# Attention woven into an expert layer on one core: key copies, exponentials and weight splits moved in the program order

## The chip, the cores and the metric

One core of a Trainium2 chip runs the whole kernel. Its engines are TensorE (PE, whose weight loads the profile lists apart as PEld), VectorE (DVE), ScalarE (ACT), GpSimd (POOL) and SyncE (SP, which here only issues DMA transfers). Each engine works through its own queue in order; semaphores tie the queues together. The metric is the device time of one execution in microseconds (us), as the median of several runs.

## The reference

Three layers follow each other (shapes: 4 batches, 8 heads, 768 positions, head size 64; 3072 tokens of 512 numbers; hidden size 2048; 8 experts of 4 slots):

```python
scores_l = scale * q @ k.T            # only |i - j| < 16 counts, the rest is masked with -1e9
scores_s = scale * q @ k_sum.T + log(32)   # k_sum: maximum of each block of 32 keys (24 blocks)
a = softmax(concat[scores_l, scores_s])
attn = a @ concat[v, v_sum]           # v_sum: mean of each block of 32 values

h = x @ w_in                          # 512 -> 2048, x = attn of all heads
g = h * cos(h)
x2 = g @ w_out                        # 2048 -> 512

logits = x2 @ phi
d = softmax(logits, over tokens);  c = softmax(logits, over slots)
out = c @ experts(d.T @ x2)           # per expert: relu(. @ w1) @ w2
```

## The kernel before

Attention is cut into 24 groups of four query windows of 64 positions and four heads (lines 622 to 650 place groups 4 to 23; groups 0 to 3 are written out ahead of the loop). The middle layer is cut into 6 blocks of 512 tokens, and each block into 16 steps of 128 hidden columns, so the main loop (line 689) has 96 steps s = 0 to 95. Four attention groups give one block's input. Block 0 needs groups 0 to 3, which run in the prologue; groups 4 to 7 run inside block 0, groups 8 to 11 inside blocks 0 and 1, and so on.

**One step.** Every product is in split form: a number is a high part that TensorE takes exactly plus a low rest. `mm1(s)` (lines 340 to 352) makes 12 matmuls of 512 columns into the PSUM tile `h`: the high weights `wih` with both parts of the input (`xh`, `xl`), then the low weights `wil` with `xh`. `act1(s)` (line 355) turns h into the cosine: two DVE operations on the tile `a` (L365, L366) and the sine on ACT (L367). `act2(s)` multiplies by h on DVE (L372), casts the high part `gh` on ACT (L375) and subtracts the low part `gl` on POOL (L376). `mm2(s-2)` (lines 379 to 393) multiplies `gh`, `gl` with the output weights `woh`, `wol`, 12 matmuls again. TensorE's queue is therefore mm1(s), mm2(s-2), mm1(s+1), mm2(s-1), with attention's small matmuls between them.

**Weights.** Both splits of step s are made by `split_w` (lines 330 to 337): a cast on ACT (L335), a subtraction on POOL (L336; in block 0 on DVE for `wi`). In block 0 each weight must first be converted from 64-bit floats: two ACT operations into `w` and `cv` (`conv_1`, L123 and L127), a shift on DVE (`conv_2`, L133), an integer addition on POOL (`conv_3`, L138).

**Attention of a group g.** `att_K` (L227) copies the block maxima of the keys `ks` behind the keys in the tile `qk`, twice 96 columns on ACT. `att_A` makes 32 score matmuls `sc` (L250) into two PSUM banks and adds scale and mask on DVE into `S` (L254). Then come the maximum (L262), the exponential, the sum, the division (`att_norm`, L290 to L293), two rounds of four transposes `tr` (`att_C`, L300) with a copy `aT` each, and `att_D`: 32 matmuls `av` (L317) whose result is split into `xh` (ACT) and `xl` (DVE). Groups 8 to 23 subtract the maximum on DVE (L266) and use one exponential for a pair of groups (`att_exp`, L271, 1920 columns). Groups 0 to 7 use `att_exps` (L283): eight exponentials of 120 columns for each group, each with its own bias and accumulated sum.

**What sets the order.** The order is written by hand. Line 690 on lists, for each step: mm1, in block 0 the conversion of a later weight, the split of `wo`, act1, the split of `wi`, what is due at position 0, act2, mm2, what is due at position 1. `at2(h, ...)` files a piece of attention under half-step h = 2s + position; the constants at the top (`HB`, `HF`, `OK`, `MC` and others) say how many half-steps a piece lies behind its group's start. All scores, transposes, `av` and block sums of values (`vs`, L181) inside the loop share two PSUM banks (the pool `ps_m`), taken in turn: a tile gets the bank of the last but one, and its first matmul waits until that one has been read. The tile `aT` has two buffers too.

Of the kernel before, what the change touches and what calls it, by code (L numbers as in the profile page):

```python
# [32 lines left out]
NF = DFF // 128  # L33
# [14 lines left out]
NRING = 7  # L48
HB = (0, 12)
HF = (-6, 10)  # L50
OA = 4
OV = 3
OK = 0
OX = 6
# [9 lines left out]
ML = 12  # L64
MC = 2
MS = 22
# [8 lines left out]
def body(ctx: ExitStack, tc: tile.TileContext, q0, qk, kT, vn, vx, w, phi, ex, cst, out):  # L75
# [187 lines left out]

    def att_sub(g):
        d = grp[g]
        nc.vector.tensor_tensor(out=d["S"], in0=d["S"],  # L266
                                in1=d["mx"].unsqueeze(2).to_broadcast([128, 8, KC]), op=ALU.subtract)
# [259 lines left out]
    def turn(g, eng=None):  # L527
        for j in range(2):
            att_C(g, j, eng or nc.vector)
# [39 lines left out]
    vsum_first()  # L569
    load_vs(0)  # L570
    load_vs(2)
    load_w(2)
    att_exps(3)
    fill(8)
    turn(0)
    load_vs(1)
    load_vs(3)
    load_w(3)
    load_qk(4)
    fill(6)  # L580
    conv_1(0)
    load_w(4)
    turn(2)
    att_norm(1, nc.gpsimd)
    fill(6)
    turn(1)
    att_norm(3, nc.gpsimd)
    conv_2(0)
    conv_3(0)
    fill(6)  # L590
    att_D(0)
    turn(3, nc.scalar)
    att_D(2)
    split_w(0, 0, nc.vector)
    att_D(1)
    att_D(3)
    conv_1(1)
    load_w(5)
    conv_2(1)
    conv_3(1)  # L600
    load_qk(5)
    att_K(4)
    split_w(1, 0, nc.vector)
    load_v(4)
    load_v(5)
    load_vs(4)
    load_vs(5)
    load_c(sel, NM + 180, 288)
    nc.sync.dma_start(out=phis.rearrange("p k s -> p (k s)"), in_=phi)

    def convert(f):
        conv_1(f)
        conv_2(f)
        conv_3(f)
        if 4 <= f < NF - 2:
            load_w(f + 2)


    for g in range(4, 24):
        h0 = HF[g // 2 % 2] + 2 * NF * (g // 4 - 1) if g > 7 else HB[g // 2 % 2]  # L620
        h = h0 + OA * (g % 2)
        n = h0 + ON + DN * (g % 2)
        if g < 8:
            if g > 5:
                at2(n - 5, load_v, g)
                at2(n - 4, load_vs, g)
                at2(h - 2, att_K, g)
            elif g == 5:
                at2(h - 1, att_K, g)
        else:  # L630
            v = n - 14 + OD2
            at2(v + 1, load_v, g)
            at2(v + 2, load_vs, g)
            at2(h - OK, att_K, g)
        at2(h, att_A, g)
        if g < 8:
            at2(h + 1, att_max, g, True)
            at2(h0 + OX, att_exps, g)
        else:
            at2(h + 1, att_max, g)  # L640
            at2(h + 1, att_sub, g)
            if g % 2:
                at2(h0 + OX, att_exp, g // 2)
            at2(h0 + OS + 2 * (g % 2), att_sum, g)
        at2(n, att_norm, g)
        at2(n + OC2, att_C, g, 0)
        at2(n + OC2 + 1, att_C, g, 1)
        at2(n + OD2, att_D, g)
        if g + 2 < 24:
            at2(h + 1, load_qk, g + 2)  # L650
# [38 lines left out]
    for s in range(NSLOT + LAG):  # L689
        if s < NSLOT:  # L690
            mm1(s)
        for f in range(2 if s == 0 else s + CL, min(s + CL + 1, NF)):
            convert(f)
        if 0 <= s - LAG + 1 < NSLOT:
            split_w((s - LAG + 1) % NF, 1)
        if s < NSLOT:
            act1(s)
        if s + 2 < NSLOT:
            split_w((s + 2) % NF, 0, nc.vector if s + 2 < NF else None)
        fire(s, 0)  # L700
        if s < NSLOT:
            act2(s)
        if s >= LAG:
            mm2(s - LAG)
            if (s - LAG) % NF == NF - 1:
                last = [x2_out(t) for t in range(4)][3]
        fire(s, 1)
        fire(s, 2)
# [242 lines left out]
```

## Time and profile before

| | us |
|---|---|
| median of 3 runs (870.97 to 871.92) | 871.5 |
| the profiled execution | 871.47 |
| its span, first to last instruction | 869.6 |
| mean granted TensorE clock | 0.94 of full speed |
| PE busy | 752.1 |
| DVE busy | 461.3 |
| ACT busy | 402.8 |
| POOL busy | 400.0 |

The profile is of one execution. Its page lists busy time of each engine, the span in 40 slices, the chain of work that ended last, and the costliest groups of instructions by line; the trace behind it answers what one engine waited for, what ran in a window, and each instruction's start and length. A granted clock of 1.00 is TensorE's 2.4 GHz level and the lower level is 1.2 GHz, so a mean of 0.86 over a window means that it was at the lower level for 28% of it. mm1 of step 0 begins at 38.72 us, of step 16 at 201.58 us, of step 64 at 586.75 us, of step 80 at 702.54 us.

### The profile page before, as it was taken

Reading aid. Unit: us, or ns where it says so; the run is one execution under the profiler, and the core shown is the slowest. Engines: PE = TensorE matmul, PEld = TensorE weight load, DVE = VectorE, ACT = ScalarE, POOL = GpSimd, SP = SyncE. Lnnn points to the kernel's source line nnn. Section 1 sums busy time; section 2 is a strip of 40 time slices with the busy share of each in tenths; the row PEclk is TensorE's granted clock in tenths of the full one; section 3 lists DMA queues with packets and bytes.
Section 4 is the critical chain, followed back from the end, with each engine's and each line's share of the span. In section 5 each row is a group of like instructions: output and inputs, shape, how many; then the busy total and the mean of one; then the engine's idle time right before and its main releaser. Section 6 shows DMA issues by size and latency. Waiting matters only on the chain.

```text
span 869.6 us, 13683 instructions
## 1 busy us (share of the span) xinstructions
PE 752.1 (86%) x5453; PEld 582.5 (67%) x5453; DVE 461.3 (53%) x688; ACT 402.8 (46%) x765; POOL 400.0 (46%) x300
## 2 busy tenths in 40 slices
PE   7847695779979979889979889889889999999995
PEld 6736474567857757767657767667667888877553
DVE  6465664656445547556446446556456544442723
ACT  5467557535524435534435524526425444443312
POOL 1355544534633734543634543746444666574000
PEclk9979799889998999999989989999999999999998
DMA  9775554132111021121111011020000282235978
GB/s 345 264 257 178 218 181 173 48 102 64 54 64 35 29 82 54 65 89 62 51 64 36 30 65 35 29 87 13 30 29 1 77 335 97 74 98 194 376 315 278
DMA packets 36304, 101.71 MB, mean 117 GB/s; under 512 B 3472, under 2 KB 14736, under 8 KB 34192
## 3 DMA queue, kind: packets, MB, share of 16 engines
q1 hardware_dynamic: 36240, 100.83, 32.9%
q8 instruction: 43, 0.70, 0.3%
q14 instruction: 21, 0.17, 0.1%
HBM read 92.17 MB, written 6.29 MB: 113 GB/s over the span
## 4 chain that ended last, share of the span: by engine, by line
PE 65%; DVE 13%; ACT 12%; issue 4%; DMA 3%; POOL 1%; SPq 0%; ACTq 0%; DVEq 0%; POOLq 0%
PE acc L388 10%; PE acc L389 9%; PE h L347 8%; PE acc L392 8%; PE h L348 7%; PE h L351 7%; DVE a L366 3%; DVE a L365 3%; PE sc L250 3%; PE av L317 3%; ACT a L367 2%; ACT wih L335 2%; PE tr L300 2%; PE yp L849 2%; PE hp L816 2%
## 5 line engine op out<-in xcount | busy, mean ns | idle before, releaser
L376 POOL TENSOR_TENSOR gl<-a,gh 128x512 fp32r<-128x512 f32 x96 | 124.1, 1292 | 147.8 <-ACT gh L375 147.8
L336 POOL TENSOR_TENSOR wil<-w,wih 128x512 fp32r<-128x512 f32 x80 | 106.9, 1337 | 175.4 <-ACT wih L335 135.7
L388 PE MATMUL acc<-woh,gh 128*128 128x512 f32 x384 | 169.9, 442 | 1.6 <-ACT gh L375 1.6
L367 ACT ACTIVATE a<-a,halfpi 128x512 f32<-128x512 f32 x96 | 69.5, 724 | 212.6 <-DVE a L366 205.0
L347 PE MATMUL h<-xh,wih 128*128 128x512 f32 x384 | 157.5, 410 | 8.8 <-DVE a L372 7.2
L389 PE MATMUL acc<-wol,gh 128*128 128x512 f32 x384 | 161.5, 420 | 0.0
L348 PE MATMUL h<-xl,wih 128*128 128x512 f32 x384 | 152.5, 397 | 0.1
L336 POOL TENSOR_TENSOR wol<-w,woh 128x512 fp32r<-128x512 f32 x96 | 128.4, 1337 | 27.7 <-ACT woh L335 27.6
L365 DVE TENSOR_SCALAR a<-h 128x512 f32<-128x512 f32 x96 | 66.0, 688 | 126.2 <-PE h L351 97.1
L375 ACT CAST gh<-a 128x512 fp32r<-128x512 f32 x96 | 59.4, 619 | 129.6 <-DVE a L372 129.6
L392 PE MATMUL acc<-woh,gl 128*128 128x512 f32 x384 | 104.7, 395 | 0.0
L351 PE MATMUL h<-xh,wil 128*128 128x512 f32 x384 | 104.3, 394 | 0.0
L388 PEld LDWEIGHTS acc<-woh,gh 128*128 128x128 f32 x384 | 79.4, 207 | 30.2 <-issue 11.5
L347 PEld LDWEIGHTS h<-xh,wih 128*128 128x128 f32 x384 | 73.2, 191 | 26.2 <-issue 8.4
L389 PEld LDWEIGHTS acc<-wol,gh 128*128 128x128 f32 x384 | 79.7, 208 | 16.4 <-issue 0.4
L392 PEld LDWEIGHTS acc<-woh,gl 128*128 128x128 f32 x384 | 74.2, 193 | 17.1
L348 PEld LDWEIGHTS h<-xl,wih 128*128 128x128 f32 x384 | 73.4, 191 | 15.2 <-DVE xl L326 0.5
L351 PEld LDWEIGHTS h<-xh,wil 128*128 128x128 f32 x384 | 72.6, 189 | 16.2
L372 DVE TENSOR_TENSOR a<-h,a 128x512 f32<-128x512 f32 x96 | 65.9, 686 | 29.7 <-ACT a L367 29.5
L250 PE MATMUL sc<-qk 64*64 64x120 f32 x640 | 30.0, 341 | 55.2 <-ACT qk L227 55.2
L366 DVE SCALAR_TENSOR_TENSOR a<-a,h 128x512 f32<-128x512 f32 x96 | 66.0, 688 | 3.3
L250 PEld LDWEIGHTS sc<-qk 64*64 64x64 f32 x640 | 23.6, 176 | 63.4 <-ACT qk L227 62.7
(128 smaller groups left out, 943.5 us busy)
## 6 DMA issues: line engine op xcount, KB each, us to landing
ex<-in_ex_dram SPq DMA_DIRECT2D x64, 512.0 KB
raw<-in_w_dram SPq DMA_DIRECT2D x16, 1024.0 KB
qk<-in_qk_dram SPq DMA_DIRECT2D x20, 736.0 KB
v<-in_vx_dram SPq DMA_DIRECT2D x24, 512.0 KB
kr<-in_kT_dram SPq DMA_DIRECT2D x16, 384.0 KB
vb<-in_vn_dram SPq DMA_DIRECT2D x12, 512.0 KB
out_dram<-o SPq DMA_DIRECT2D x12, 512.0 KB
v<-vs SPq DMA_DIRECT2D x48, 48.0 KB
```

The source lines that it names most:

```text
L250: nc.tensor.matmul(pss[hh][o, c:c + KC], t[:, 0:QB], t[:, QB:], start=True, stop=True)
L336: (eng or nc.gpsimd).tensor_tensor(out=lo, in0=W[f][:, part, :], in1=hi, op=ALU.subtract)
L347: nc.tensor.matmul(h, hi[:, c], xh[s // NF][:, t, :], start=t == 0, stop=False)
L348: nc.tensor.matmul(h, hi[:, c], xl[s // NF][:, t, :], start=False, stop=False)
L351: nc.tensor.matmul(h, lo[:, c], xh[s // NF][:, t, :], start=False, stop=t == 3)
L365: nc.vector.tensor_scalar(out=a, in0=h, scalar1=0.25, scalar2=MAGIC, op0=ALU.add, op1=ALU.add)
L366: nc.vector.scalar_tensor_tensor(out=a, in0=a, scalar=MAGIC, in1=h, op0=ALU.subtract, op1=ALU.subtract)
L367: nc.scalar.activation(a, a, AF.Sin, bias=halfpi, scale=-TWO_PI)
L376: nc.gpsimd.tensor_tensor(out=gl, in0=a, in1=gh, op=ALU.subtract)
L388: nc.tensor.matmul(acc[t], gh[:, c], hi, start=f == 0, stop=False)
L389: nc.tensor.matmul(acc[t], gh[:, c], lo, start=False, stop=False)
L392: nc.tensor.matmul(acc[t], gl[:, c], hi, start=False, stop=f == NF - 1)
```

## The change

- **Key copies** (`att_K`) of groups 8 to 23 are filed three half-steps ahead of their scores (`OK` from 0 to 3). In block 0 those of groups 6 and 7 are too, that of group 5 two half-steps.
- **Activation first.** In every step act1 comes directly behind mm1. The splits of both weights, and in block 0 the conversions, come behind mm2; the output weights of step s are split in step s instead of s+1. A conversion is cut into its ACT half and its DVE and POOL half, one step apart.
- **One exponential per pair** for groups 4 to 7, as groups 8 to 23 have it: the subtraction goes to POOL, the sum to DVE; the pieces are placed anew (`HB` from (0, 12) to (2, 13), and new offsets).
- **Prologue.** The second weight is converted earlier, the normalisations on POOL come earlier, loads are listed in another order, the filler matmuls (`fill`) are dealt out otherwise.
- `MC` from 2 to 3: `m2_c`, the transposition `dt` of the token weights, one half-step later.

```diff
-HB = (0, 12)
+HB = (2, 13)
-OK = 0
+OK = 3
-MC = 2
+MC = 3
...
-    def att_sub(g):
+    def att_sub(g, eng=None):
         d = grp[g]
-        nc.vector.tensor_tensor(out=d["S"], in0=d["S"],
+        (eng or nc.vector).tensor_tensor(out=d["S"], in0=d["S"],
...
+    def convert(f, parts):
+        if 1 in parts and f < NF:
+            conv_1(f)
+            if 4 <= f < NF - 2:
+                load_w(f + 2)
+        if 2 in parts and f < NF:
+            conv_2(f)
+            conv_3(f)
...
         if g < 8:
             if g > 5:
...
+                at2(h - 3, att_K, g)
+            elif g == 5:
                 at2(h - 2, att_K, g)
...
+            at2(h, att_A, g)
+            at2(h + 1, att_max, g)
+            at2(h + 1, att_sub, g, nc.gpsimd)
+            if g % 2:
+                at2(h0 + 7, att_exp, g // 2)
+            n = h0 + 9 + g % 2
+            at2(n, att_sum, g)
+            at2(n + 1, att_norm, g)
+            n = h0 + 12 + 2 * (g % 2)
+            at2(n, att_C, g, 0)
+            at2(n + 1, att_C, g, 1)
+            at2(h0 + 15 + 2 * (g % 2), att_D, g)
         else:
...
-        for f in range(2 if s == 0 else s + CL, min(s + CL + 1, NF)):
-            convert(f)
-        if 0 <= s - LAG + 1 < NSLOT:
-            split_w((s - LAG + 1) % NF, 1)
-        if s < NSLOT:
+            if s == 0:
+                convert(2, (2,))
             act1(s)
-        if s + 2 < NSLOT:
-            split_w((s + 2) % NF, 0, nc.vector if s + 2 < NF else None)
         fire(s, 0)
         if s < NSLOT:
             act2(s)
...
+        if s == 0:
+            convert(3, (1,))
+        if s + 2 < NSLOT:
+            split_w((s + 2) % NF, 0, nc.vector if s + 2 < NF else None)
+        convert(s + 3, (2,))
+        if s < NSLOT:
+            split_w(s % NF, 1)
+        convert(s + 4, (1,))
         fire(s, 1)
```

How the queues change, at the places that matter below. ACT's queue in step 21, in which group 10's scores are made (`a21` is the sine of step 21, `qk10` the key copies of group 10), before:

```order
L335 CAST woh4_2158<-w4_697 128x512
L367 ACTIVATE a21_2162<-a21_2162,halfpi_90 128x512
L335 CAST wih7_2166<-w7_895 128x512
L227 COPY qk10_1663<-ks4_724 128x4x24
L227 COPY qk10_1663<-ks5_806 128x4x24
L375 CAST gh21_2196<-a21_2162 128x512
L326 CAST xh2_2063<-av9_2212 128x2x256
```

And ACT's queue with the change, from the end of step 19 to the end of step 21:

```order
L227 COPY qk10_1619<-ks4_733 128x4x24
L227 COPY qk10_1619<-ks5_793 128x4x24
L367 ACTIVATE a20_2070<-a20_2070,halfpi_90 128x512
L306 COPY aT9_0_2079<-tr9_0_2074 120x512
L375 CAST gh20_2092<-a20_2070 128x512
L335 CAST wih6_2108<-w6_787 128x512
L335 CAST woh4_2112<-w4_661 128x512
L306 COPY aT9_1_2121<-tr9_1_2116 120x512
L417 COPY x2T_1816<-xt_2123 128x512
L367 ACTIVATE a21_2142<-a21_2142,halfpi_90 128x512
```

The copies stood behind the sine of the scores' own step; now they stand ahead of the sine of the step before, and `wih` and `woh` behind `gh`.

DVE's queue in step 6 of block 0, where group 6's scores (`sc6`) are read into `S6` and the second block sum of values (`vs1_1`, which takes the bank of `sc6_0`) is added, before:

```order
L365 TENSOR_SCALAR a6_1044<-h6_1019 128x512
L366 SCALAR_TENSOR_TENSOR a6_1044<-a6_1044,h6_1019 128x512
L336 TENSOR_TENSOR wil8_1049<-w8_953,wih8_1048 128x512
L290 TENSOR_SCALAR sm5_852<-sm5_852 128x8
L292 RECIPROCAL rs5_1053<-sm5_852 128x8
L293 TENSOR_TENSOR S4_652<-S4_652,rs5_1053 128x960
L254 SCALAR_TENSOR_TENSOR S6_1056<-sc6_0_1057,mask_85 128x480
L254 SCALAR_TENSOR_TENSOR S6_1056<-sc6_1_1058,mask_85 128x480
```

And with the change:

```order
L290 TENSOR_SCALAR sm4_983<-sm4_983 128x8
L292 RECIPROCAL rs4_1016<-sm4_983 128x8
L293 TENSOR_TENSOR S4_686<-S4_686,rs4_1016 128x960
L276 TENSOR_REDUCE sm5_1019<-S4_686 128x8
L372 TENSOR_TENSOR a6_1011<-h6_998,a6_1011 128x512
L336 TENSOR_TENSOR wil8_1039<-w8_920,wih8_1038 128x512
L133 TENSOR_SCALAR w9_977<-w9_977 128x1024
L290 TENSOR_SCALAR sm5_1019<-sm5_1019 128x8
L292 RECIPROCAL rs5_1055<-sm5_1019 128x8
L293 TENSOR_TENSOR S4_686<-S4_686,rs5_1055 128x960
L254 SCALAR_TENSOR_TENSOR S6_1058<-sc6_0_1059,mask_85 128x480
L254 SCALAR_TENSOR_TENSOR S6_1058<-sc6_1_1060,mask_85 128x480
```

Both pieces are followed, in either order, by the addition of `vs1_1`. Behind the two operations on `a6` and ahead of the two reads of the score banks there stand now both divisions of the pair, a sum, the product of step 6, a split and a shift, where there were one split and one division.

## Rows read from the trace of the kernel before

**Rows 1.** The page's chain of work that ended last: share of the span by engine.
```profile
PE 65%; DVE 13%; ACT 12%; issue 4%; DMA 3%; POOL 1%; SPq 0%; ACTq 0%; DVEq 0%; POOLq 0%
```

**Rows 2.** Busy time in windows: from, to and length, then per engine, clock, DMA.
```profile
38.72:201.58 162.86, 115.24 (x764) 89.88 (x761) 94.85 (x128) 96.40 (x188) 78.58 (x48) 0.86 0.46 162
201.58:702.54 500.96, 451.72 (x2953) 354.40 (x2952) 276.42 (x401) 224.88 (x390) 248.72 (x191) 0.95 0.16 54
702.54:803.90 101.36, 101.36 (x527) 80.48 (x525) 40.83 (x66) 43.96 (x77) 62.51 (x49) 1.00 0.41 143
803.90:869.60 65.70, 53.58 (x661) 29.98 (x659) 27.47 (x56) 18.46 (x38) 0.00 (x0) 0.94 0.87 321
319.69:331.10 11.41, 8.34 (x57) 6.51 (x56) 5.52 (x8) 4.06 (x9) 6.00 (x5) 0.85 0.21 69
713.61:719.14 5.53, 5.53 (x25) 4.50 (x24) 3.26 (x6) 3.34 (x7) 3.82 (x3) 1.00 0.26 95
```

**Rows 3.** What PE waited for: us in total, times, longest.
```profile
PE sc L250 <- ACT qk L227: 55.2, 17, 5.9
PE tr L300 <- DVE S L293: 21.6, 3, 9.2
PE dt L462 <- ACT e L450: 2.6, 3, 0.9
```

**Rows 4.** Timeline of step 31: start, length, instruction [idle before it].
```profile
322.73 0.69 DVE L365 TENSOR_SCALAR a<-h 128x512 f32<-128x512 f32 x1 [2.10 <-PE h L351]
323.45 0.69 DVE L366 SCALAR_TENSOR_TENSOR a<-a,h 128x512 f32<-128x512 f32 x1
324.24 0.72 ACT L367 ACTIVATE a<-a,halfpi 128x512 f32<-128x512 f32 x1 [2.44 <-DVE a L366]
324.87 0.60 ACT L335 CAST wih<-w 128x512 fp32r<-128x512 f32 x1
325.37 0.44 ACT L227 COPY qk<-ks 128x96 f32<-128x96 f32 x2
325.69 1.88 PE L250 MATMUL sc<-qk 64*64 64x120 f32 x32 [3.07 <-ACT qk L227]
...
328.76 0.68 DVE L372 TENSOR_TENSOR a<-h,a 128x512 f32<-128x512 f32 x1
...
329.47 0.62 ACT L375 CAST gh<-a 128x512 fp32r<-128x512 f32 x1 [3.66 <-DVE a L372]
```

**Rows 5.** Groups by line: busy us, mean ns, idle before and its releasers.
```profile
L336 POOL TENSOR_TENSOR wol<-w,woh 128x512 fp32r<-128x512 f32 x96 | 128.4, 1337 | 27.7 <-ACT woh L335 27.6
L376 POOL TENSOR_TENSOR gl<-a,gh 128x512 fp32r<-128x512 f32 x96 | 124.1, 1292 | 147.8 <-ACT gh L375 147.8
L138 POOL TENSOR_TENSOR w<-w,cv 128x1024 int32<-128x1024 int32 x16 | 38.2, 2388 | 21.4 <-ACT cv L127 17.2 <-DVE w L133 2.3 <-ACT woh L335 1.8
L293 POOL TENSOR_TENSOR S<-S,rs 128x960 f32<-128x960 f32 x4 | 7.4, 1856 | 26.3 <-DVE rs L292 26.3
L293 DVE TENSOR_TENSOR S<-S,rs 128x960 f32<-128x960 f32 x20 | 25.5, 1277 | 0.7
L262 DVE TENSOR_REDUCE mx<-S 128x8 f32<-128x960 f32 x24 | 27.5, 1144 | 0.1
L336 DVE TENSOR_TENSOR wil<-w,wih 128x512 fp32r<-128x512 f32 x16 | 17.4, 1090 | 24.9 <-ACT wih L335 24.9
L133 DVE TENSOR_SCALAR w<-w 128x1024 int32<-128x1024 int32 x16 | 13.1, 817 | 25.1 <-ACT w L123 25.1
L123 ACT ACTIVATE w<-raw 128x1024 f32<-128x1024 f32 x16 | 18.2, 1138 | 0.0
L283 ACT ACTIVATE S<-S,mx 128x120 f32<-128x120 f32 x64 | 24.3, 380 | 9.3 <-DVE mx L262 9.3
L283 ACT ACT_TABLE_LOAD x2 | 2.6, 1283 | 0.0
L271 ACT ACTIVATE S<-S 128x1920 f32<-128x1920 f32 x8 | 14.5, 1808 | 0.1
```

More of the change, by code (lines that the diff above doesn't have):

```diff
@@ L569, in body @@
     vsum_first()
-    load_vs(0)
-    load_vs(2)
+    for g in (0, 2, 1, 3):
+        load_vs(g)
     load_w(2)
+    load_qk(4)
+    load_w(3)
     att_exps(3)
+    att_norm(1, nc.gpsimd)
     fill(8)
     turn(0)
[L576 to L579, printed above, removed]
     fill(6)
@@ L582, in body @@
     load_w(4)
+    conv_1(1)
+    load_w(5)
     turn(2)
-    att_norm(1, nc.gpsimd)
-    fill(6)
+    att_norm(3, nc.gpsimd)
+    fill(8)
     turn(1)
-    att_norm(3, nc.gpsimd)
     conv_2(0)
     conv_3(0)
-    fill(6)
     att_D(0)
+    fill(4)
     turn(3, nc.scalar)
@@ L594, in body @@
     split_w(0, 0, nc.vector)
+    conv_2(1)
+    conv_3(1)
     att_D(1)
     att_D(3)
[L597 to L600, printed above, removed]
     load_qk(5)
-    att_K(4)
-    split_w(1, 0, nc.vector)
     load_v(4)
@@ L607, in body @@
     load_vs(5)
+    split_w(1, 0, nc.vector)
+    conv_1(2)
+    att_K(4)
     load_c(sel, NM + 180, 288)
     nc.sync.dma_start(out=phis.rearrange("p k s -> p (k s)"), in_=phi)
[L611 to L616, printed above, removed]
+    def convert(f, parts):
[6 more added lines that the diff above has]
+            conv_3(f)
     for g in range(4, 24):
@@ L624, in body @@
             if g > 5:
-                at2(n - 5, load_v, g)
-                at2(n - 4, load_vs, g)
+                at2(h0 + 5 + 2 * (g % 2), load_v, g)
+                at2(h0 + 7 + 2 * (g % 2), load_vs, g)
+                at2(h - 3, att_K, g)
+            elif g == 5:
                 at2(h - 2, att_K, g)
-            elif g == 5:
-                at2(h - 1, att_K, g)
+            at2(h, att_A, g)
[10 more added lines that the diff above has]
+            at2(h0 + 15 + 2 * (g % 2), att_D, g)
         else:
@@ L634, in body @@
             at2(h - OK, att_K, g)
[L635 to L639, printed above, removed]
+            at2(h, att_A, g)
             at2(h + 1, att_max, g)
@@ L644, in body @@
             at2(h0 + OS + 2 * (g % 2), att_sum, g)
[L645 to L648, printed above, removed]
+            at2(n, att_norm, g)
+            at2(n + OC2, att_C, g, 0)
+            at2(n + OC2 + 1, att_C, g, 1)
+            at2(n + OD2, att_D, g)
         if g + 2 < 24:
```

## The prediction

> **What bounds the kernel now.** I read first the chain of work that ended last [rows 1]: PE carries 65% of it, DVE and ACT a quarter together, so PE is the resource and the other two interrupt it. Then the windows [rows 2] say where. Block 5, steps 80 to 95, has no attention: PE is busy for all of its 101.36 us at clock 1.00, and one of its steps takes 5.53. Blocks 1 to 4 are one window of 500.96 us, with PE idle for 49.2 (500.96 - 451.72) and the clock at 0.95, which is worth up to 25 more (0.05 x 501). Block 0 (38.72 to 201.58) is worst: 162.86 us, 47.6 of it idle, clock 0.86. The tail of 65.7 us stays as it is. Third, the waits of PE [rows 3]: 55.2 us in 17 waits are score matmuls that wait for the key copies on ACT; 21.6 in three are transposes that wait for a division on DVE, all in block 0.
>
> **The key copies, groups 10 to 23.** The timeline of step 31 shows one such wait [rows 4]. PE ends mm1, and the scores stand next. Their copy stands on ACT behind the sine of the same step, the sine behind two DVE operations on the h that mm1 has just made: 0.69 + 0.69 + 0.72, a split, the copies, and PE starts 3.07 us late. The scores then take 1.88. The row of the whole step [rows 2] gives the price: 11.41 us with PE busy for 8.34, so 3.07 idle, at clock 0.85, which costs 0.15 x 11.41 = 1.7: together 4.8. With the change the copies lie ahead of the sine of the step before, whose inputs are older by a whole step. The two copies are the only instructions that this moves; they need keys loaded some twelve half-steps earlier, so I see no new wait for SP's queue. There are 14 such steps from step 16 on: 14 x 4.8 = **67 us**. From below it is 14 x 3.07 = 43, if the slow clock stayed; from above 49.2 + 25 = 74, if all waiting went. I take 67, since block 5 shows that PE without waits runs at 1.00.
>
> What is late next there? In these steps the rest of the order moves too: `wih` and `woh` stand behind `gh`. Counted from the end of mm1(s): a 1.4, sine 2.1, product 2.8, `gh` 3.4, `wih` of step s+2 4.0 [rows 4], then POOL `gl` 4.7, `wil` 6.0, `wol` 7.4 at 1.3 each [rows 5]. PE needs `wih` of s+2 after three pieces of 2.77 (half a step of 5.53), at 8.3, and `wol` of s at 11.1. That is 4.3 and 3.7 us to spare; an exponential with its table loads (1.28 + 1.81 [rows 5], plus three small ones of some 0.9) takes 4.0 of it in one step of eight, and the second table load 1.28 of the next. So `wih` fits, and `wol` is up to 0.3 late in such a step, 2 us in eight of them, which I set off against the next term. POOL works 3.9 us a step.
>
> **Small waits in blocks 1 to 4.** Of the 49.2 idle, 14 x 3.07 = 43 are key copies; 6 remain, among them `dt` behind its exponential, 2.6 [rows 3], which `MC` moves by 2.8 us. I take **3 us**, bounds 0 and 6.
>
> **Prologue and block 0.** Here gains and new waits mix, so I followed the new queues by hand with the durations of rows 4 and 5. The prologue converts the second weight earlier and does not wait for the division of group 1: mm1(0) starts at about 36 instead of 38.7, mm1(2) at 49 instead of 55. Without waits block 0 would take 16 times what a step of blocks 1 to 4 costs PE, (451.7 - 25) / 64 = 6.67, so 107, less some 3 for the token weights that it lacks: 104.
>
> Eight exponentials a group (16 x 0.38 = 6.1 a pair) become one of 1.81: 4.3 less on ACT for each of two pairs, with the same table loads of 1.28. In exchange POOL subtracts (4 x 1.86, bounded by 1.28 from DVE's division and 1.86 from POOL's), DVE sums (4 x 1.14). With the conversion POOL then does 1.29 + 2.39 + 1.34 = 5.0 in a step and 6.9 in a step with a subtraction, PE 5.53. DVE and ACT form a ring in each of these steps, since the sine of s+1 stands behind the split of s: sine 0.72, product 0.69, `gh` 0.62, `wih` 0.60, `wil` 1.09, shift 0.82, a 1.38, together 5.9, plus 1.14 with a maximum. So block 0 does not become PE-bound, and PE meets these waits:
> - step 2, 5.4: its first weight stands behind a conversion, a shift, POOL's addition and the sine's table load;
> - steps 3 to 5, 4: a key copy and twice `wol` behind POOL's addition;
> - step 6, 13.5: group 6's scores need the bank that `vs` of step 5 leaves after a sum, which waits for the pair's exponential (4.8). Then `vs1_1` needs the bank of `sc6_0`, which DVE reads only after two divisions of some 2.1, a sum 1.14, a product 0.69, a split 1.09, a shift 0.82 and the ACT casts between, so 8.7 more;
> - step 8, 5.5: the scores of group 7 need the bank of `av`, whose cast stands behind ACT's conversion of 2 x 1.14;
> - step 12, 3.6 (the new place of the wait for a division, once 9.2); step 13, 7.4, when group 8's scores need two banks held by transposes whose copies stand behind the sine of step 13; steps 14 and 15, 3.
>
> Sum 42.4, and the slow clock after the four long ones 1.7 each, 7. So mm1(16) starts at 36 + 104 + 42.4 + 7 = 189.4 instead of 201.6: **12 us** gained. Bounds: nothing (201.6), and 36 + 107 + a few = 150 if my waits are covered.
>
> One rule speaks against the new subtraction. DVE's split `wil` averages 1.09 where its equals on 512 columns take 0.69 [rows 4, 5]: something lengthens it, and POOL works beside it. The Trainium skill (GPSIMD Engine Reference, Engine selection and Key points) advises VectorE for elementwise work, as GpSimd is about two times slower for two inputs and shares its SBUF interfaces with VectorE. The trace bears out less: POOL's 1.86 against DVE's 1.28 for the same division is 1.45 times [rows 5]. By the rule four subtractions would cost 4 x 2.56, 2.8 us more than I count, and the sum would be 792.
>
> **The sum.** 67 + 3 + 12 = 82 off the profiled execution's 871.47, which equals the median of 871.5 within 0.03: **789 us**. A difference within 0.2% is what a measurement of this kernel can't tell from none.
>
> **Rivals.**
> - *A, the clock stays down.* Small waits remain before attention's pieces in all blocks, and PE doesn't come back to the upper level: only 43 of the 67 come, 813 us. For it: step 31 stayed slow beyond its wait. Against: steps between two waits run at full speed already, as block 5 does. 0.06.
> - *B, block 0 gives nothing.* The bank waits in steps 6 and 13 are longer than I found, or DVE is held up by POOL, and mm1(16) starts at 202 to 210: 801 to 809 us. For it: every operation is behind another in these queues. 0.13.
> - *C, block 0 runs near PE's pace*, because ACT and DVE catch up in the light steps: mm1(16) at 160 to 175, 760 to 775 us. For it: 8.6 us less on ACT and three waits of 7 us gone. Against: the ring of 5.9. 0.13.
> - *D, the wait moves.* PE no longer waits for the copies, but for banks that DVE frees after scale and mask; half of 67 comes, 823 us. Against: those reads stand directly behind the two operations on a. 0.04.
> - *E, slower.* With `wih` behind `gh` and mm2, ACT delivers it after PE is due in every step. The point of decision is 4.3 us of lag on ACT beyond what I add up; with x us more than that, each of 80 steps stretches by x, and at x = 1.3 the 104 us outweigh all gains: 893 us. Against: ACT is busy for 225 of 501 us in blocks 1 to 4 [rows 2]. 0.02.
> - *F, no change*: the copies are done earlier but waits elsewhere take all of it, 871 us. 0.01.
>
> **How the numbers follow.** The forecast itself, 778 to 800, has 0.61. The range goes from 766 to 809: it takes in B and half of C, leaving out A, D, E, F (0.13) and 0.065 of C. Faster by over 0.2%: everything but E and F, 0.97; within 0.2%: 0.01; slower: 0.02.
>
> **What would show it.** Right: the wait of scores for key copies falls from 55.2 to under 5 us; the window of blocks 1 to 4 shrinks to about 431 at clock 0.98 or more; the tail and block 5 keep 65.7 and 101.4; block 0 still has 40 us of idle PE, with waits of `vs` in step 6 and of scores in steps 8 and 13. Wrong: a clock under 0.96 in blocks 1 to 4 (A), scores that wait for DVE (D), first matmuls of steps that wait for `wih` (E), mm1(16) before 178 or after 200 (C, B).

## The result, and the profile after

The changed kernel takes **806.6 us** (median of 4 runs, 804.3 to 807.7) against 871.4 before: a ratio of 0.925, 95% interval 0.923 to 0.927, so 64.8 us less. The forecast was 789, the range 766 to 809. The profiled execution took 806.3 us, its span is 804.5, its granted clock 0.961. The windows of the trace after, for the stretches of [rows 2]: block 0, blocks 1 to 4, block 5, tail.

```profile
36.33:200.42 164.09, 119.58 (x764) 92.47 (x761) 103.11 (x132) 85.85 (x124) 86.83 (x52) 0.84 0.46 168
200.42:637.53 437.11, 430.54 (x2954) 337.46 (x2952) 284.05 (x401) 225.45 (x389) 252.90 (x191) 1.00 0.19 63
637.53:738.80 101.27, 101.27 (x526) 80.44 (x525) 40.09 (x66) 44.33 (x76) 62.59 (x49) 1.00 0.41 144
738.80:804.50 65.70, 53.64 (x662) 30.02 (x660) 27.53 (x56) 18.50 (x38) 0.00 (x0) 0.94 0.88 321
```

Nearly all of the gain is in the second row: 500.96 has become 437.11, with PE idle for 6.6 instead of 49.2 and the clock at 1.00. Block 5 and the tail are as before. Block 0 is 1.2 us longer than before (164.09 against 162.86), and begins 2.4 earlier, so that step 16 starts at 200.42 instead of 201.58. The waits of PE answer to [rows 3]:

```profile
PE vs L181 <- DMA vb<-in_vn_dram: 8.9, 2, 8.2
PE vs L181 <- DVE S L254: 8.1, 1, 8.1
PE sc L250 <- ACT aT L306: 8.0, 3, 3.9
PE tr L300 <- DVE S L293: 7.8, 5, 4.4
PE h L347 <- ACT wih L335: 5.1, 1, 5.1
PE acc L389 <- POOL wol L336: 3.5, 3, 2.0
PE sc L250 <- ACT qk L227: 2.8, 1, 2.8
```

The 55.2 us of scores that waited for key copies are 2.8, in one wait. The chain that ended last [rows 1] has less of ACT in it, 7% instead of 12, and more of DMA, 7% instead of 3:

```profile
PE 67%; DVE 15%; ACT 7%; DMA 7%; issue 3%; SPq 1%; DVEq 0%; ACTq 0%
```

Step 31, the step of [rows 4], in the timeline after (start, length, engine, line):

```profile
297.70 0.45 ACT L227 COPY qk<-ks 128x96 f32<-128x96 f32 x2
302.38 0.72 ACT L367 ACTIVATE a<-a,halfpi 128x512 f32<-128x512 f32 x1 [4.23 <-DVE a L366]
302.74 0.40 PE L347 MATMUL h<-xh,wih 128*128 128x512 f32 x1
305.60 1.05 PE L250 MATMUL sc<-qk 64*64 64x120 f32 x32
306.58 0.50 PE L388 MATMUL acc<-woh,gh 128*128 128x512 f32 x1
```

The copies are done 7.5 us before the scores (305.60 - 297.70 - 0.45), ahead of the sine. The scores follow mm1 without a gap and take 1.05 instead of 1.88. The costliest groups that answer to [rows 5] (line, engine, operation, count, busy us, mean ns, idle before):

```profile
L293 DVE TENSOR_TENSOR S<-S,rs 128x960 f32<-128x960 f32 x20 | 36.0, 1802 | 0.7
L276 DVE TENSOR_REDUCE sm<-S 128x8 f32<-128x960 f32 x20 | 22.8, 1142 | 12.2 <-ACT S L271 12.2
...
L266 POOL TENSOR_TENSOR S<-S,mx 128x960 f32<-128x960 f32 x4 | 7.2, 1796 | 14.8 <-DVE mx L262 14.8
```

The sums (1.14) and the subtractions on POOL (1.80) are near what was counted (1.14 and 1.86). The division on DVE is not: 1.80 on average instead of 1.28.

**Where block 0 went.** The chain of waits, in the stretch that holds its two longest (start, length, what):

```profile
75.36 0.87 DVE ks L167
76.25 6.29 DMA kr<-in_kT_dram
82.57 0.96 DVE ks L167
83.55 5.44 DMA vb<-in_vn_dram
89.12 1.08 PE vs L181 x16
...
97.71 1.06 DVE sm L276
98.78 0.61 DVE a L372
...
101.93 0.60 DVE w L133
102.89 3.08 DVE S L293
105.97 0.58 DVE S L254
106.59 1.08 PE vs L181 x16
```

Two different rings are in it, each a circle in which a piece waits for one that in its turn waited for the piece before. The first five rows are SP's: raw keys `kr` and raw values `vb` of batch 1 share one buffer (tag `v2`), so a load can be issued only when the one before has been reduced; each round takes load plus reduction, 6.29 + 0.96, and PE waits 8.2 us for the load that it needs in its own queue. The rest is the wait that was foreseen: `vs` needs a bank of group 6's scores, which DVE reads (L254) only behind sum, product, shift and division.

SP's part is longer than this stretch. Earlier in the same chain stand:

```profile
36.82 12.00 DMA v<-in_vx_dram
...
53.74 5.95 DMA kr<-in_kT_dram
59.72 0.96 DVE ks L167
60.70 6.39 DMA kr<-in_kT_dram
```

SP's queue waits for the load of `v` to land before it issues the copies into `v` (at 48.83), and the loads `kr` stand behind these. Added up over block 0, the chain has 36.1 us of DMA and 4.9 of SP's issues, beside 51.9 of PE, 45.2 of DVE and 21.2 of ACT. In the kernel before it had 5.4 of DMA, 46.4 of PE, 41.1 of DVE and 43.5 of ACT. So in this chain ACT lost 22 us, and the loads and SP's issues gained 36. SP's queue also keeps its own time: in the nine profiles with the new prologue mm1(0) starts at 33.5 to 36.3 us, but the first of these `kr` loads is issued at 53.2 to 54.6 in all of them.

### The profile page after: what moved, and what is told of

It is laid out like the page before. It is cut to its first block, busy times and chain, and to the rows that moved or that the text cites. A ratio compares the mean times of both kernels' runs of the same rounds, so it can differ in the third digit from the quotient of the medians.

```text
span 804.5 us, 13755 instructions
## 1 busy us (share of the span) xinstructions
PE 735.0 (91%) x5453; PEld 567.9 (71%) x5453; DVE 476.4 (59%) x692; ACT 395.3 (49%) x703; POOL 412.3 (51%) x304
## 3 DMA queue, kind: packets, MB, share of 16 engines
HBM read 92.17 MB, written 6.29 MB: 122 GB/s over the span
## 4 chain that ended last, share of the span: by engine, by line
PE 67%; DVE 15%; ACT 7%; DMA 7%; issue 3%; SPq 1%; DVEq 0%; ACTq 0%
PE acc L388 9%; PE h L347 9%; PE h L348 8%; PE acc L389 8%; PE h L351 8%; PE acc L392 8%; DVE S L293 3%; DMA kr<-in_kT_dram 3%; PE av L317 3%; PE tr L300 2%; PE sc L250 2%; DVE a L366 2%; DVE a L365 2%; PE yp L861 2%; ACT S L271 2%
## 5 line engine op out<-in xcount | busy, mean ns | idle before, releaser
L347 PE MATMUL h<-xh,wih 128*128 128x512 f32 x384 | 160.8, 419 | 5.2 <-ACT wih L335 5.1
L388 PE MATMUL acc<-woh,gh 128*128 128x512 f32 x384 | 159.0, 414 | 1.7 <-ACT gh L375 1.7
L389 PE MATMUL acc<-wol,gh 128*128 128x512 f32 x384 | 153.2, 399 | 3.5 <-POOL wol L336 3.5
L348 PE MATMUL h<-xl,wih 128*128 128x512 f32 x384 | 155.1, 404 | 0.6 <-DVE xl L326 0.6
L336 POOL TENSOR_TENSOR wil<-w,wih 128x512 fp32r<-128x512 f32 x80 | 111.8, 1398 | 1.0 <-ACT wih L335 1.0
L388 PEld LDWEIGHTS acc<-woh,gh 128*128 128x128 f32 x384 | 73.4, 191 | 26.8 <-issue 9.4
L372 DVE TENSOR_TENSOR a<-h,a 128x512 f32<-128x512 f32 x96 | 65.8, 686 | 39.4 <-ACT a L367 39.4
L389 PEld LDWEIGHTS acc<-wol,gh 128*128 128x128 f32 x384 | 73.6, 192 | 19.7 <-POOL wol L336 4.8
L392 PEld LDWEIGHTS acc<-woh,gl 128*128 128x128 f32 x384 | 72.3, 188 | 16.3
L335 ACT CAST woh<-w 128x512 fp32r<-128x512 f32 x96 | 59.2, 616 | 3.0 <-PE acc L392 3.0
L335 ACT CAST wih<-w 128x512 fp32r<-128x512 f32 x96 | 59.1, 616 | 2.6 <-POOL w L138 2.6
```

Of the source, the lines that this page charges most:

```text
L335: nc.scalar.copy(hi, W[f][:, part, :])
L336: (eng or nc.gpsimd).tensor_tensor(out=lo, in0=W[f][:, part, :], in1=hi, op=ALU.subtract)
L347: nc.tensor.matmul(h, hi[:, c], xh[s // NF][:, t, :], start=t == 0, stop=False)
L348: nc.tensor.matmul(h, hi[:, c], xl[s // NF][:, t, :], start=False, stop=False)
L388: nc.tensor.matmul(acc[t], gh[:, c], hi, start=f == 0, stop=False)
L389: nc.tensor.matmul(acc[t], gh[:, c], lo, start=False, stop=False)
```

## The experiments

All stand against the kernel before on the same chip. Block 0 is the stretch from the first matmul of mm1(0) to that of mm1(16) in the one profiled execution of each.

| kernel | us | ratio, 95% interval | mm1(0) | mm1(16) | block 0 |
|---|---|---|---|---|---|
| before | 871.4 | | 38.72 | 201.58 | 162.9 |
| the change | 806.6 | 0.925 (0.923 to 0.927) | 36.33 | 200.42 | 164.1 |
| e1 keys alone | 799.6 | 0.917 (0.913 to 0.922) | 38.84 | 198.53 | 159.7 |
| e2 all but the keys | 861.1 | 0.989 (0.983 to 0.994) | 35.07 | 198.84 | 163.8 |
| e3 keys one half-step | 805.9 | 0.926 (0.921 to 0.930) | 35.20 | 198.97 | 163.8 |
| e4 old pieces, new order | 802.9 | 0.922 (0.918 to 0.926) | 34.48 | 195.82 | 161.3 |
| e5 value sums later | 800.2 | 0.919 (0.915 to 0.923) | 33.81 | 194.49 | 160.7 |
| e6 pair exponential, old order | 795.8 | 0.914 (0.911 to 0.917) | 37.68 | 190.99 | 153.3 |
| e7 subtraction on DVE | 811.1 | 0.930 (0.926 to 0.934) | 33.98 | 202.00 | 168.0 |
| e8 two waits taken away | 799.6 | 0.918 (0.914 to 0.922) | 33.54 | 193.49 | 160.0 |
| e9 later transposes, old order | 800.1 | 0.916 (0.914 to 0.919) | 39.13 | 193.47 | 154.3 |
| e10 waits filled with matmuls | 805.2 | 0.922 (0.919 to 0.925) | 34.90 | 199.69 | 164.8 |
| e12 e6 with subtraction on POOL | 791.7 | 0.907 (0.904 to 0.911) | 38.41 | 187.63 | 149.2 |
| e13 old offsets, new order | 799.5 | 0.915 (0.913 to 0.918) | 33.49 | 193.89 | 160.4 |

mm1(0) moves by up to 3 us between profiles of kernels with one and the same prologue (33.5 to 36.3), so the length of block 0 is what I compare; it charges an early start for what does not come earlier with it, such as SP's loads. Two profiles are of an execution at the edge of its kernel's runs: e1's is its slowest (803.1), e7's its fastest (807.4). The experiments ran on three chips, where the medians of the kernel before are 871.4 to 872.6.

**e1, the key copies alone.** The kernel before with one constant changed:

```diff
-OK = 0
+OK = 3
```

> The kernel before with one number changed: the key copies of groups 8 to 23 three half-steps ahead. Theory (the copies carry the gain, whatever the rest of the order): blocks 1 to 4 shrink from 501 to 434 to 442 us at a clock of 0.98 or more, as with the whole change (437), and the copies of groups 8 and 9 in steps 13 and 15 give 6 to 12 us more in block 0, so 795 to 803 us, faster than the whole change (806.6). Rival (the activation-first order is needed, since with the splits ahead of the sine PE meets other waits once the copies are gone): at least 20 of the 64 us are missing, 825 us or more.

Measured 799.6, as the theory had it: more than the whole change gives. Its windows, block 0 and blocks 1 to 4:

```profile
38.84:198.53 159.69, 115.36 (x764) 89.55 (x761) 93.77 (x127) 96.41 (x188) 77.40 (x47) 0.84 0.45 159
198.53:634.05 435.52, 429.35 (x2954) 337.62 (x2952) 280.32 (x402) 225.16 (x391) 255.51 (x192) 1.00 0.19 64
```

Blocks 1 to 4 lose 65.4 us by that one number. The rest of the change costs about 7 us on top of it.

**e2, all but the key copies.** The changed kernel with the copies of groups 8 to 23 back in front of their scores:

```diff
-OK = 3
+OK = 0
```

> The change with the key copies of groups 8 to 23 put back directly ahead of their scores; all else as changed. Theory: 16 waits of some 3.1 us come back with the slow clock behind them, 4.6 each in blocks 1 to 4 and up to 4 each in steps 13 and 15: 870 to 882 us. Rival: the new order of sine and splits carries part of the gain by itself: under 850 us.

Measured 861.1: below the 870 to 882 of the theory, and above the 850 of the rival. In its profile blocks 1 to 4 are still 11.5 us shorter than before:

```profile
198.84:688.26 489.42, 447.23 (x2953) 349.60 (x2952) 282.43 (x401) 226.79 (x389) 253.74 (x191) 0.97 0.17 56
```

and among its waits of PE is

```profile
PE sc L250 <- ACT qk L227: 46.0, 17, 4.8
```

The wait for the copies is 46.0 instead of 55.2, since no weight split stands between sine and copies any more. So the two parts overlap: the new order shortens the very waits that the keys take away, and its gain in blocks 1 to 4 is gone once the keys are ahead.

**e3, how far ahead.** The changed kernel with `OK = 1`.

```diff
-OK = 3
+OK = 1
```

> The change with those copies one half-step ahead of the scores instead of three: they stand behind the casts of the step before and still ahead of the sine of the scores' own step. Theory (what counts is only that the copy stands ahead of that sine): within 0.4% of 806.6 us, scores wait for the copies 4 us or less in all. Rival (the lead counts, as the copies end late behind the two weight casts): PE waits 1 us or more in each of 14 steps, 820 us or more.

Measured 805.9, with 4.5 us of scores that wait for copies, within the noise of the change itself. The theory held: what counts is that the copies are ahead of their own step's sine, and further ahead gives nothing that these runs can tell.

**e4, e13 and e6: order and pieces apart.** e4 keeps the new prologue and loop order, and gives groups 4 to 7 the pieces and offsets of before (`HB = (0, 12)`):

```diff
-            at2(h + 1, att_max, g)
-            at2(h + 1, att_sub, g, nc.gpsimd)
...
+            at2(h + 1, att_max, g, True)
+            at2(h0 + OX, att_exps, g)
+            at2(n, att_norm, g)
```

> The changed kernel, but groups 4 to 7 keep the pieces and offsets of before (eight exponentials a group, no subtraction, no sum on DVE). Theory: what block 0 lost in the change lies in the new attention pieces (the wait for the load of vb behind the sums of the values, 8.2 us, and for the bank behind DVE's division, 8.1 us), so without them mm1(16) starts at 190 to 196 instead of 200.4 and the time is 796 to 802, as with the key copies alone (799.6) or a little less. Rival: the new order of the loop itself (conversion and splits behind mm2) is what costs, and the pieces give what they should, 4.3 us less on ACT for each pair: mm1(16) at 200 to 208, 807 to 815.

e6 is e1 with one exponential per pair, at the offsets of before:

```diff
-        if g < 8:
-            at2(h + 1, att_max, g, True)
-            at2(h0 + OX, att_exps, g)
-        else:
...
+        at2(h + 1, att_max, g)
+        at2(h + 1, att_sub, g)
+        if g % 2:
+            at2(h0 + OX, att_exp, g // 2)
+        at2(h0 + OS + 2 * (g % 2), att_sum, g)
```

> The kernel before with the key copies ahead, as the first experiment (799.6), and one exponential per pair for groups 4 to 7 at the offsets of before, with the subtraction on DVE. Theory: the pieces by themselves give back as much as they save: ACT loses 4.3 us a pair, DVE gets 1.3 and 1.1 us a group, and the transposes already wait for a division on DVE (21.7 us in three); 799 to 806, mm1(16) at 198 to 205. Rival: they save their 8.6 us on ACT, and only in the new order do they cost: 791 to 796, mm1(16) at 190 to 194.

e13 is e4 with the same pieces as e6:

```diff
-            at2(h + 1, att_max, g, True)
-            at2(h0 + OX, att_exps, g)
+            at2(h + 1, att_max, g)
+            at2(h + 1, att_sub, g)
+            if g % 2:
+                at2(h0 + OX, att_exp, g // 2)
+            at2(h0 + OS + 2 * (g % 2), att_sum, g)
```

> The new order of the loop and prologue, with one exponential per pair at the offsets of before and the subtraction on DVE: the fourth corner of old or new order by eight exponentials or one per pair. Theory: the parts add up; what cost in the changed kernel are its new offsets (sums, scores and divisions on top of the waits for the sums of the values): 802.9 - (799.6 - 795.8) = 799, between 797 and 801. Rival: in the new order DVE stands before the splits and cannot bear the subtraction and the sum, whatever the offsets: 804 to 809.

e4 fits neither text well: 802.9 lies between the two, with mm1(16) at 195.8 in the theory's band. e6 came out at 795.8 with mm1(16) at 191.0, in its rival's bands: the pieces save time by themselves. e13's theory held, 799.5 against 799. With all four corners, in medians:

| | eight exponentials a group | one per pair, old offsets |
|---|---|---|
| old order | 799.6 (e1) | 795.8 (e6) |
| new order | 802.9 (e4) | 799.5 (e13) |

The exponential gives 3.8 and 3.4, the new order costs 3.3 and 3.7. The gain of the exponential is clear of the scatter: the runs of e6 (795.7 to 796.9) all lie below those of e1 (797.9 to 803.1), those of e13 (796.8 to 800.3) below those of e4 (802.0 to 803.9). The cost of the new order is not: the runs of e1 and e4 overlap, and those of e6 and e13 touch. The profiles show it in larger numbers: block 0 of e13 is 7.1 longer than that of e6, and begins 4.2 earlier with the new prologue. (e13 has `MC = 3` and the earlier key copies of groups 5 to 7 too.) PE's longest waits in block 0 (a view of that stretch) of e6:

```profile
PE tr L300 <- DVE S L293: 13.0, 3, 5.4
PE h L347 <- DVE a L372: 7.2, 1, 7.2
```

and of e13:

```profile
PE h L347 <- ACT wih L335: 11.6, 4, 3.5
PE vs L181 <- DMA vb<-in_vn_dram: 9.1, 2, 6.2
```

The new order exchanges waits for the division and for a PSUM bank of `h` against two others: mm1 waits four times for its weight split `wih`, which now stands behind mm2, and the sums of values wait for their loads. As I read the order, these are late because the reductions of keys that free their buffer now stand on DVE behind the conversion and the splits; that was not tried by itself.

**e5 and e8, the two long waits.** In e5 the loads `vb` of batch 1 are summed later:

```diff
-                at(i, 1, load, *k)
-                at(i + 1, 1, use, *k)
+                lo, us = ((i, 1), (i + 1, 1)) if i < 4 else (((4, 1), (6, 0)), ((6, 0), (8, 0)), ((8, 0), (9, 1)))[i - 4]
+                at(*lo, load, *k)
+                at(*us, use, *k)
```

> The change with the three block sums of values of the second batch later, at steps 6, 8 and 9 and, for the first two, ahead of the product with the output weights, instead of at the ends of steps 5, 6 and 7; their loads are issued one step and more before. Theory: both waits of some 8 us, for the load in step 5 and for the score bank in step 6, go, and what DVE and ACT have queued comes into view behind them: mm1(16) at 187 to 194 instead of 200.4, 793 to 801 us. Rival (block 0 is set by the queues of DVE and ACT, and PE only waits elsewhere): mm1(16) at 197 or later, 803 us or more.

In e8 they get buffers of their own, and two more pieces move:

```diff
+        if b == 1:
+            pool, tag, n = wres, f"w{12 + i}", 1
...
-                at2(h - 2, att_K, g)
+                at2(h - 4, att_K, g)
...
-            at2(n + 1, att_norm, g)
+            at2(n + 1 + g % 2, att_norm, g)
...
+                lo, us = ((i, 1), (i + 1, 1)) if i < 4 else (((2, 1), (4, 0)), ((3, 1), (5, 0)), ((4, 1), (7, 0)))[i - 4]
```

> The changed kernel with what ends its two longest waits of block 0 moved: the weights vb of batch 1 get buffers of their own and their loads are issued in steps 2 to 4, their sums done in steps 4, 5 and 7; the keys of group 5 to 7 are copied one half-step earlier; the division of the second group of a pair stands half a step later, behind the reads of the banks of the scores. Theory: the waits of vs for its load (8.2 us) and for the bank (8.1) go, up to 3 us of them come back at the next pieces, and the clock recovers 1 to 2: mm1(16) at 186 to 191, 792 to 797. Rival: the ring of DVE and ACT (5.9 us a step) sets the pace whatever these waits do: mm1(16) at 196 to 200, 801 to 806.

e5 gained 6.4 us and e8 7.0, in block 0 itself 3.4 and 4.1, out of the 16.3 of the two waits. In e5 the bank wait is gone, but 5.4 of the wait for the load remain; its time is at the theory's upper edge, its mm1(16), 194.5, just above it. In e8 the bank wait is gone and the load's is down to 1.8, so 14.5 us went, but new waits are there (its lines are two higher):

```profile
PE sc L252 <- ACT aT L308: 10.1, 2, 6.2
PE h L349 <- ACT wih L337: 8.8, 2, 5.1
...
PE vs L183 <- DVE mx L264: 5.5, 1, 5.5
```

e8 lies between its theory (792 to 797) and its rival (801 to 806), and nearer to what the rival says: by the length of block 0, some 70% of what went comes back at the next pieces (10.4 of 14.5), by the medians about half.

**e10, the waits filled.** Matmuls that nobody reads, so that PE works while it waits:

```diff
+    def keep(ps, n):
+        for i in range(n):
+            nc.tensor.matmul(ps[:, 0:128], ones, ones, start=True, stop=True)
...
+        if s == 2:
+            keep(h, 14)
...
+        if (b, i) == (1, 0):
+            keep(ps, 24)
...
+        if (g, j) == (6, 0):
+            keep(ps, 12)
```

> The changed kernel with extra matmuls that nobody reads, put where PE waits with its own bank free: 14 ahead of mm1(2) (wait 5.1), 24 ahead of the first sum of values of batch 1 (8.2), 12 ahead of the transposes of group 6 (4.4). They are begun while PE waits. Theory: what block 0 costs above its work and its waits is slow clock that these waits bring: the steps behind them had PE busy for 7.4 us at clock 0.79, 9.3 at 0.70, 12.7 at 0.65, and at full clock these would be 1.5, 2.8 and 4.4 shorter; PE busy of block 0 less the extra matmuls falls from 119.6 to 111 to 115, mm1(16) starts at 192 to 197, the time is 798 to 803. Rival: the clock falls on account of the short waits that stay, or PE's longer matmuls come from other work beside them; mm1(16) at 199 to 203, 805 to 810.

Measured 805.2, the rival's number. The windows of step 6 and step 13 in the changed kernel:

```profile
90.14:107.60 17.46, 9.33 (x76) 7.04 (x72) 13.93 (x18) 6.84 (x9) 10.02 (x6) 0.70 0.41 151
...
163.61:180.40 16.79, 12.71 (x66) 9.79 (x65) 10.92 (x17) 5.35 (x10) 6.45 (x5) 0.65 0.08 24
```

and in e10 all of block 0 and the same two steps:

```profile
34.90:199.69 164.79, 128.57 (x864) 102.67 (x861) 102.95 (x132) 85.98 (x124) 86.83 (x52) 0.88 0.47 172
90.07:107.22 17.15, 9.04 (x77) 6.79 (x73) 13.79 (x18) 6.74 (x9) 9.88 (x6) 0.80 0.44 155
162.54:179.71 17.17, 10.56 (x67) 8.14 (x66) 11.30 (x17) 5.36 (x11) 6.88 (x5) 0.70 0.08 24
```

The extra matmuls (L172 of e10) by themselves in block 0, PE and PEld:

```profile
34.90:199.69 164.79, 13.39 (x100) 13.19 (x100) 0.88 0.47 172
```

The clock did rise (0.84 to 0.88), and PE's own work fell from 119.6 to 128.6 - 13.4 = 115.2 us. Yet the block is as long as before: step 13 has 2.1 us less of PE work and ends no sooner. What PE saves it waits. The extra matmuls have a price of their own: they take 13.4 us where the three waits shrank by 11.3 (5.1 to 1.9, 8.2 to 2.9, 4.4 to 1.6), and in step 2 mm1 begins 1.6 us after its weight is there. That is some 2 us at most, less than the 4.4 that PE saved. So neither of the two texts has the reason quite: the slow clock is real, and it is not what block 0 costs.

**e7 and e12, where the subtraction stands.** e7 is the changed kernel with it on DVE:

```diff
-            at2(h + 1, att_sub, g, nc.gpsimd)
+            at2(h + 1, att_sub, g)
```

> The changed kernel with the four subtractions of block 0 on DVE instead of POOL. Theory: DVE's division beside POOL took 3.08 us instead of 1.16 because POOL held it up, in the very chain that ends the 8.1 us wait for the bank of the scores of group 6. POOL's part goes over to DVE at 1.2 us each; that chain gets 1 to 3 us shorter, and mm1(16) starts at 197 to 200: 803 to 806. Rival: DVE is the bound of block 0 and pays 4 x 1.2 more, and nothing comes back: mm1(16) at 203 to 206, 809 to 812.

e12 is e6 with it on POOL:

```diff
-        at2(h + 1, att_sub, g)
+        at2(h + 1, att_sub, g, nc.gpsimd if g < 8 else None)
```

> The fastest kernel so far (old order, keys ahead, one exponential per pair: 795.8) with the four subtractions of block 0 on POOL, as the changed kernel has them. Theory: what held in the changed kernel (806.6 with them on POOL, 811.1 on DVE) holds in the old order too, since DVE is in the ring of block 0 and POOL is not: 795.8 - 4.5 = 791, between 789 and 793, mm1(16) at 185 to 189. Rival: in the old order POOL's weight split wol, which PE waits for, and the conversions stand behind the subtraction, and the exponential starts later by POOL's longer time: 796 to 801, mm1(16) at 191 to 196.

Measured 811.1 and 791.7: POOL is the better place by 4.5 and 4.1 us (block 0: 3.9 and 4.1), in both orders; on DVE the four take 7.1 us in e7 and 6.2 in e6. So more than half of DVE's time counts in block 0, and POOL's (7.2 us for the four in the change) much less. My theory for e7 fell and e12's held; the division is as long with the subtraction on DVE as with it on POOL (means of the four in block 0: 2126 and 2124 ns), since what it collides with is another POOL operation (last section). e12 is the fastest kernel of the study, 7.9 us below e1. The length of block 0 makes 10.5 of the 11.2 us between their two profiled executions, and blocks 1 to 4 are as long as e1's:

```profile
38.41:187.63 149.22, 114.34 (x763) 88.26 (x761) 99.40 (x131) 87.56 (x126) 87.61 (x51) 0.89 0.49 171
187.63:623.10 435.47, 429.29 (x2953) 337.64 (x2952) 280.33 (x402) 225.21 (x391) 255.24 (x192) 1.00 0.19 63
```

**e9, two waits moved by a half-step.** e6 with the transposes and products of groups 4 and 6 one half-step later, and `MC = 3`:

```diff
+        c = int(g in (4, 6))
+        at2(n + OC2 + c, att_C, g, 0)
+        at2(n + OC2 + 1 + c, att_C, g, 1)
+        at2(n + OD2 + c, att_D, g)
```

> As the kernel with one exponential per pair in the old order (795.8), with the transposes of groups 4 and 6 and their last products one half-step later, and the transposition of block statistics (dt) one later (MC = 3). Theory: the two waits of 5.3 us of transposes for a division lose a half-step, 2.7 us each, and the 2.6 us of dt behind its exponential go: 795.8 - 5.4 - 2.6 = 788, between 786 and 791, mm1(16) at 184 to 187. Rival: the products that follow wait instead, or the time comes back at the next piece, as in the changed kernel: 793 to 797, mm1(16) at 189 to 192.

Measured 800.1, 4 us slower than e6: a miss, beyond the rival too. The two waits of 5.3 are gone, and `wol` (8.6 us in five waits instead of 2.0 in two), a load of values (3.9) and scores behind `aT` (6.5 instead of 2.5) take their place. The wait of `dt` went too, and blocks 1 to 4 are no shorter for it. Here too waits of block 0 went, and the block did not get shorter (154.3 against 153.3). Of the 3.5 us between the two profiled executions 1.5 lie ahead of block 0, where the two kernels are the same, so only a part of the 4 us is shown to be e9's doing.

## Why the prediction was right, and where it was wrong

The range holds, by 2.4 us, and so do the sign and the place of the gain. The forecast does not: 806.6 is 17.6 us above 789 and outside the 778 to 800 that the prediction thought likeliest. The range takes it in only because it was widened for rival B. Two terms make the difference: mm1(16) starts at 200.4 instead of 189.4 (11.0), and blocks 1 to 4 take 437.1 instead of 431.0 (6.1).

- **Key copies and small waits, 67 + 3: right in mechanism, too large by 6.** 63.9 us came in blocks 1 to 4, 65.4 with the keys alone. Idle PE fell by 42.7, as predicted for the copies (43). The excess is in two terms. PE's busy time fell by 21.2, where I had 14 x 1.7 = 24. And of the 6 us of small waits, half of which I counted as a gain, as much remains: `dt` no longer waits, but transposes wait for divisions (3.4 us in four waits), and PE is idle for 6.6. e2 shows that the change's other parts are worth 11.5 us there only as long as the copies are late.
- **Clock, rival A: fell.** Blocks 1 to 4 run at 1.00 although small waits are left.
- **What is late next, rivals D and E: fell as stated for blocks 1 to 4.** No step there begins with a wait for `wih`, and no scores wait for DVE. In block 0 a small form of E is real: e13 waits 11.6 us for `wih` where e6 waits 1.6.
- **Prologue: right in sign, and in size partly by luck.** mm1(0) at 36.3 and mm1(2) at 49.4, predicted 36 and 49. In the eight other profiles with this prologue mm1(0) starts at 33.5 to 35.2, in those with the old one at 37.7 to 39.1.
- **Block 0, 12 us: this step failed; 1.2 came.** Most of the single waits were found well: 5.4 in step 2 (measured 5.1), 8.7 for the bank of group 6's scores (8.1), 5.5 in step 8 (3.9), a wait for a division in step 12 (4.4), banks in step 13 (3.2 and 0.9). Their sum, 42.4, even meets PE's idle time, 164.09 - 119.58 = 44.5. But that is partly luck: the 8.2 us for the load of `vb` were in no line of mine, because I had followed the queues of ACT, DVE and POOL and left out SP's, with one buffer for seven loads in turn, the 4.8 foreseen for the scores of group 6 did not show, and step 13 came out 3.3 smaller. The surcharge for the slow clock was 7; PE was busy for 119.6 us instead of my 104, so 15.6, if 104 was right.
- **The reason behind both: the sum itself.** I took block 0 as PE's work plus PE's waits plus slow clock, as if each could be had on its own. That holds in blocks 1 to 4, where PE sets the pace. In block 0 it doesn't: e10 took 4 us of work off PE and the length stayed, e8 took 14.5 us off two waits and got 4.1, e9 took away two of 5.3 and got nothing. What sets the pace there instead is shown in part only. The ring of DVE and ACT that the prediction worked out, 5.9 us a step, makes 94 us in 16 steps, far from 164, so it is not that ring alone. The chain that ended last goes through DVE, ACT, PE and the loads by turns, and not the same way in each kernel: in block 0 it has 45 us of DVE and 36 of DMA in the change, 71 and 12 in e7, 28 and 6 in e12. I read this as several queues of nearly the same length beside each other, so that one that is shortened leaves another; that DVE's is one of them e7 and e12 show, that SP's is one rests on the chain and on e5 and e8. What I should have summed is what the change adds to and takes off each queue, SP's included. The medians give the parts along one path, which closes by itself (another order of the parts could divide the sum otherwise), from the 799.6 of e1: one exponential per pair -3.8 (e6 against e1), the new order of prologue and loop +3.7 (e13 against e6), the new offsets +11.6 (e7 against e13), the subtraction on POOL -4.5 (the change against e7); together 806.6. In the single profiles the offsets are 7.6 of block 0 (168.0 against 160.4; e7's execution is its fastest, 3.7 below its median), and the new order is a start 4.2 earlier against 7.1 more in block 0 and 1.6 more in blocks 1 to 4 (437.2 in e13, 435.6 in e6). I had predicted the exponential with the right sign, and taken the order and the offsets to be free but for the waits that I found.
- **The subtraction on POOL: better than either price.** I weighed 1.86 by the trace against 2.56 by the rule; e7 and e12 show that it pays 4 us, since it takes time off DVE's queue. By the trace the factor of two is nearer than the prediction's 1.45: the 1.28 was a mean with collisions in it (last section), and alone DVE's division takes 1.16 against 1.86, 1.6 times, its split 0.69 against POOL's 1.30, 1.9 times. The Trainium skill's advice for DVE (GPSIMD Engine Reference, Engine selection) would have cost those 4 us here.
- **Rival B, block 0 gives nothing**, is what happened, nearly: mm1(16) at 200.4 is past the 200 that was to show it, though under its band of 202 to 210, and the time is in its 801 to 809 only with the 6.1 us missing from blocks 1 to 4. Of its two reasons, longer bank waits are not there. DVE held up by POOL is seen in the trace (below), but no run shows that it cost the 12 us.

What stays open: which queue holds block 0 at each place, and why the new offsets cost 11.6 us (7.6 in the profiles' block 0), were not taken apart further, and of e9's loss only the new waits are known, not what started them.

## What to carry to other kernels

Before adding up waits, ask in each stage which queue sets the pace: where it is not the engine whose waits are listed, most of a wait that is removed can come back at the next piece, and one has to count what the change adds to each queue instead. In a stage full of pieces on shared buffers, follow the DMA queue too: a single buffer for several loads is a ring of its own, here of 7 us a round. And a change of several parts is tried part by part: here one constant gave 71.8 us, two more parts some 4 each, and the rest took some 15 back.

## What the runs showed of the hardware

A DVE operation that reads two SBUF tensors (tiles that do not lie in PSUM) and a POOL operation did not run side by side. Timeline of the changed kernel, two places:

```profile
79.82 1.30 POOL L376 TENSOR_TENSOR gl<-a,gh 128x512 fp32r<-128x512 f32 x1
80.29 1.37 DVE L336 TENSOR_TENSOR wil<-w,wih 128x512 fp32r<-128x512 f32 x1 [1.21 <-ACT wih L335]
...
102.61 2.34 POOL L138 TENSOR_TENSOR w<-w,cv 128x1024 int32<-128x1024 int32 x1 [1.23 <-DVE sm L290]
102.89 3.08 DVE L293 TENSOR_TENSOR S<-S,rs 128x960 f32<-128x960 f32 x1
104.91 2.20 POOL L336 TENSOR_TENSOR wol<-w,woh 128x512 fp32r<-128x512 f32 x1
```

The division begins while POOL adds the parts of a weight, and ends 1.02 us after it (105.97 against 104.95), about the 1.16 that it takes alone (mean of the four in block 0 of e6). POOL's next operation, often 1.30, takes 2.20 and ends 1.14 after the division. `wil` takes 1.37 beside a `gl` that began first, and 0.69 where no POOL operation runs (as at 40.33). Where `wil` begins first (116.36 against 116.39), it takes 0.69 and `gl` 1.83. L372, whose one input lies in PSUM, has the same size and keeps a mean of 0.69 over all 96. The Trainium skill has the rule (SBUF — State Buffer, Terms): VectorE and GpSimd arbitrate for a shared pair of ports, held for a full instruction, and the loser "fully blocks". These rows agree with it: the rest of POOL's 2.34 (2.06) plus the division's own 1.16 make 3.22, near the 3.08. So the 1.09 that the prediction saw for `wil` and left as "something lengthens it" is this, and the mean division of the changed kernel, 1.80 instead of 1.28, is it too: two divisions of block 0 stand beside the conversion (3.08 and 3.10), and 11 of the 16 in blocks 1 to 4 take some 1.98 beside a weight split, where 13 of 16 took 1.16 before. How much of block 0's 164 us that makes was not measured by itself.
